# Two PSUM tiles of the first transposes trade places, and one more operand split on VectorE, in a fused attention and two feed-forward layers

## The chip, the cores and the metric

The kernel runs on one core of one Trainium2 chip. The metric is device time in microseconds (us), the median of three runs. A core has TensorE (PE: matmuls; PEld: the loading of their weights), VectorE (DVE), ScalarE (ACT), GpSimd (POOL) and SyncE (SP, which here issues nearly all DMAs). Matmul results land in PSUM, which has eight banks of 128 partitions by 512 float32 values.

## The reference

Float32 data of 2 batches, 12 heads, 448 positions and 64 values a head; 896 tokens of 768 values behind the attention.

```
# attention, for each batch and head
scores = cap * tanh((q @ k.T / sqrt(64)) / cap)
attn   = exp(scores - max); attn = attn / (sum(attn) + 1e-9)
x      = attn @ v                        # heads side by side: 896 x 768
# first feed-forward, d_ff 1024
h    = x @ w_in
solu = h * softmax(h)
ln   = (solu - mean(solu)) / sqrt(var(solu) + 1e-6) * g_ln
x2   = ln @ w_out
# second feed-forward, d_ff 1536
out  = (silu(x2 @ w_gate) * (x2 @ w_val)) @ w_out2
```

## The kernel before, in words

Every matmul operand is split into two parts, hi (a rounded copy, made by an ACT Copy or a DVE CAST) and lo (the remainder, a DVE subtraction), and a product is three matmuls: hi by hi, hi by lo, lo by hi. The attention goes over 12 pairs of heads (6 in each batch). For pair `i`, `attn_T` (L198) transposes q and k on TensorE into PSUM and writes their hi and lo parts to the tile `ks_i`; `attn_qk` (L222) makes the scores `sc` in four chunks, each followed by a tanh on ScalarE into the tile `P`; one exp over all of `P`; `attn_sums` (L243) makes the softmax sums in the tile `S_i`; `attn_pv` (L268) multiplies with v; `attn_norm` (L279) writes the split result to the tile `x`. `attn_pair` (L290) interleaves them: scores of pair `i`, transposes of pair `i+1`, sums and values of pair `i-1`, and beside them the conversion of one slice of `w_in` (tile `wi`, on VectorE). In this part each engine runs its instructions in the order in which the code is written.

Before the first pair, TensorE runs 18 small matmuls on zeros (`keep_warm`, L174, tile `warm`); then the seven transposes of q of pair 0 (tile `T_q`), two more zero matmuls, and the seven of k (`T_k`). The hi parts of pair 1's k and q are made on VectorE, those of all other pairs on ScalarE.

The attention's PSUM is two pools. The pool of the scores has banks 0 to 3 (two tiles of two banks). The other, `ptA`, has one slot for each tag: `pv`, `S` and `t`. A slot is as large as the largest tile of its tag (two banks for `t`, since `T_1` and all later pairs take k and q in one tile of two banks), and the slots lie in the order in which the tags are first used. `pv` comes first (the zero matmuls write into it), then `S` (for `T_q`), then `t` (for `T_k`): in the built program `pv` is bank 4, `S` bank 5, `t` banks 6 and 7.

The first feed-forward goes over seven blocks of 128 tokens. `ff1_h` (L357) makes `h` of a block in 36 matmuls, alternating between two halves of 512 columns. Its `tail` follows: on VectorE the maximum (TENSOR_REDUCE), on ScalarE the exp, on VectorE the product with `h` (SCALAR_TENSOR_TENSOR, the last reader of `h`), the statistics, one step on GpSimd, and a TENSOR_SCALAR that writes the normalised block to the tile `e`. `ff1_T` (L422) then transposes `e` (tiles `lt`). The order on TensorE is: `h` of block 0, `h` of block 1, `lt` of block 0, `h` of block 2, `lt` of block 1, and so on. `h` of block 0 starts inside the attention's last pair and takes a tile of the tag `t` (`htag`). From block 1 on, both PSUM pools are given back and one pool of eight single banks is used; a tile in it waits for whatever last used its bank. In the built program, of before and of the change, it gives the halves of block 1 banks 0 and 7, the two `lt` tiles of block 0 banks 6 and 5, and the halves of block 2 banks 4 and 3.

Of the kernel before, what the change touches and what calls it, by code (L numbers as in the profile page):

```python
# [5 lines left out]
F32 = mybir.dt.float32  # L6
# [30 lines left out]
class Kernel:  # L37
# [160 lines left out]
    def attn_T(self, i):  # L198

        CP, S = self.CP, self.S  # L200
        r = self.raws[i]
        ks = r["ks"] = self.at.tile([128, 2, 2, S], F32R, name=f"ks_{i}", tag="ks", bufs=2)
        if i:
            ps = self.pt.tile([128, 2, 512], F32, name=f"T_{i}", tag="t")
            lots = [(ps, "kq", S)]
        else:
            ps = [self.pt.tile([128, 512], F32, name=f"T_{n}", tag=t) for n, t in (("q", "S"), ("k", "t"))]
            lots = [(p.unsqueeze(1), n, w) for p, n, w in zip(ps, "qk", (S, CP))]
        for ps, names, w in lots:
            for c in range(7):  # L210
                for j, n in enumerate(names):
                    a = slice(0, 64) if n == "k" else slice(64, 128)
                    self.transpose(ps[:, j, c * 64:(c + 1) * 64], r["kq"][a, c * 128:(c + 1) * 128], self.ident[a, a])
            m = slice("kq".index(names[0]), "kq".index(names[-1]) + 1)
            for a in (slice(0, w), slice(w, S)):
                if a.start < a.stop:
                    (self.hi_dve if i == 1 else self.hi_act)(ks[:, m, 0, a], ps[:, :, a])
                    self.lo_dve(ks[:, m, 1, a], ps[:, :, a], ks[:, m, 0, a])
            if names == "q":
                self.keep_warm(2)  # L220

    def attn_qk(self, i, c):  # L222

# [444 lines left out]
```

## Time and profile before

| | |
|---|---|
| median of 3 runs | 507.58 us (506.9 to 508.31) |
| the profiled execution, its own time | 507.78 us |
| its span, first to last instruction | 506.0 us |
| TensorE busy | 493.0 us (97%) |
| VectorE busy | 352.3 us (70%) |
| ScalarE busy | 248.7 us (49%) |

The span is what the trace shows; the execution's own time has 1.78 us around it. Busy shares are means over stages with different limits: about 112 us of attention, then the first feed-forward to about 241 us, then the second to the end.

### The profile page before, as it was taken

The page shows a single profiled execution, that of the slowest core. Times are in us where ns is not written, and L with a number is a line of the kernel's source. Part 1 is how long each engine was busy: PE and PEld are TensorE (multiplying, and loading weights), DVE is VectorE, ACT ScalarE, POOL GpSimd, SP SyncE. Part 2 cuts the span into 40 slices and gives each one's busy share as a digit, 9 for nine tenths or more (in the row PEclk, how much of TensorE's full clock was granted, in tenths as well). Part 3 has the DMA queues.
Part 4 walks back from the last instruction along what each step waited for, and adds up shares of the span by engine and source line. Part 5 has one row for each costly group of instructions (what it writes and reads, how often), then busy time and mean ns, then how long its engine had stood idle before and what let it go on. Part 6 is the DMA issues. An engine that isn't in the chain of part 4 may idle for free.

```text
span 506.0 us, 7801 instructions
## 1 busy us (share of the span) xinstructions
PE 493.0 (97%) x3112; PEld 406.6 (80%) x3112; DVE 352.3 (70%) x634; ACT 248.7 (49%) x362; POOL 21.8 (4%) x62
## 2 busy tenths in 40 slices
PE   8999999995999999999999999999999999999997
PEld 7544454544888899988999988899999889999996
DVE  2799999975387896668899989897997868200000
ACT  5999999841212697466544444343444434100000
POOL 1111111110000000000000000000000000000000
PEclk9999999998899999999999999999999999999999
DMA  6865655220000232145444544534343534000000
GB/s 148 214 164 145 151 143 138 62 79 6 0 1 0 72 95 82 46 127 185 145 160 133 177 135 145 168 126 149 105 152 95 155 96 155 32 31 32 31 33 31
DMA packets 66694, 52.42 MB, mean 104 GB/s; under 512 B 35681, under 2 KB 62049, under 8 KB 66657
## 3 DMA queue, kind: packets, MB, share of 16 engines
q1 hardware_dynamic: 66624, 51.92, 35.4%
q8 instruction: 24, 0.39, 0.3%
q14 instruction: 14, 0.11, 0.1%
q0 software_dynamic: 32, 0.00, 0.0%
HBM read 49.16 MB, written 2.75 MB: 103 GB/s over the span
## 4 chain that ended last, share of the span: by engine, by line
PE 93%; ACT 5%; DVE 1%; issue 0%; ACTq 0%
PE o L29 17%; PE g L29 17%; PE v L29 17%; PE h L29 12%; PE x L29 11%; PE pv L29 7%; PE sc L29 6%; ACT P L29 4%; PE S L29 4%; PE lt L29 1%; PE warm L29 1%; DVE sm L29 1%; ACT e L29 0%; DVE e L29 0%; ACT wo L29 0%
## 5 line engine op out<-in xcount | busy, mean ns | idle before, releaser
L29 PE MATMUL g<-x,y 128*128 128x512 f32 (+1 forms) x432 | 91.2, 363 | 0.0
L29 PE MATMUL v<-x,y 128*128 128x512 f32 (+1 forms) x432 | 90.5, 362 | 0.0
L29 PEld LDWEIGHTS g<-x,y 128*128 128x128 f32 x432 | 78.4, 188 | 8.9
L29 PEld LDWEIGHTS v<-x,y 128*128 128x128 f32 x432 | 78.2, 188 | 8.5
L29 PE MATMUL h<-wi,x 128*128 128x512 f32 x252 | 61.3, 403 | 5.5 <-DVE e L29 5.5
L29 PEld LDWEIGHTS h<-wi,x 128*128 128x128 f32 x252 | 48.4, 194 | 17.0 <-DVE e L29 5.9
L29 PE MATMUL o<-x,a 128*128 128x384 f32 x294 | 52.3, 334 | 0.0
L29 PEld LDWEIGHTS o<-x,a 128*128 128x128 f32 x294 | 51.1, 188 | 0.0
L29 ACT ACTIVATE P<-sc,consts 112x896 f32<-112x896 f32 x48 | 45.9, 1012 | 6.2 <-PE sc L29 6.1
L29 PE MATMUL sc<-ks 64*112 64x448 f32 x288 | 38.8, 387 | 2.5 <-ACT P L29 1.1
L29 ACT ACTIVATE P<-P,consts 112x3584 f32<-112x3584 f32 x12 | 39.5, 3289 | 0.4
L517 ACT ACTIVATE ob<-o 128x384 f32<-128x384 f32 x14 | 6.9, 490 | 64.6 <-PE o L29 64.6
L29 PE MATMUL pv<-P,v 112*32 112x448 f32 x384 | 38.3, 539 | 0.0
L29 PEld LDWEIGHTS sc<-ks 64*112 64x112 f32 x288 | 22.4, 171 | 19.2 <-ACT P L29 8.3
L29 PE MATMUL x<-lB,wo 128*128 128x256 f32 (+1 forms) x192 | 37.3, 338 | 0.4 <-ACT lB L29 0.4
L29 PE MATMUL o<-y,a 128*128 128x384 f32 x189 | 34.1, 334 | 0.0
L29 PEld LDWEIGHTS o<-y,a 128*128 128x128 f32 x189 | 32.9, 188 | 0.1
L29 PEld LDWEIGHTS x<-lB,wo 128*128 128x128 f32 x192 | 30.1, 189 | 3.6 <-ACT lB L29 0.6
L29 PEld LDWEIGHTS pv<-P,v 112*32 112x32 f32 x384 | 12.4, 110 | 23.9 <-issue 23.1
L29 PE MATMUL x<-lA,wo 128*128 128x384 f32 x144 | 28.5, 336 | 0.0
L29 PEld LDWEIGHTS x<-lA,wo 128*128 128x128 f32 x144 | 25.2, 188 | 1.1
L29 DVE SCALAR_TENSOR_TENSOR w<-w_raw,w 128x768 uint32<-128x768 uint32 (+1 forms) x26 | 23.1, 891 | 0.3
(96 smaller groups left out, 623.5 us busy)
## 6 DMA issues: line engine op xcount, KB each, us to landing
wg_raw<-in_moe_w_gate_dram SPq DMA_DIRECT2D x12, 768.0 KB, 4.2
wv_raw<-in_moe_w_val_dram SPq DMA_DIRECT2D x12, 768.0 KB, 4.2
w_raw<-in_moe_w_out_dram SPq DMA_DIRECT2D x11, 768.0 KB, 4.4
wi_raw<-in_moe_w_in_dram SPq DMA_DIRECT2D x12, 512.0 KB, 5.0
wo_raw<-in_moe_w_out_dram SPq DMA_DIRECT2D x12, 512.0 KB, 3.5
kq<-in_q_dram SPq DMA_DIRECT2D x24, 112.0 KB, 4.6
kq<-in_k_dram SPq DMA_DIRECT2D x24, 112.0 KB, 2.7
v<-in_v_dram SPq DMA_DIRECT2D x24, 112.0 KB, 2.6
```

The source lines that it names most:

```text
L29: i = f(*a, **k)
L517: nc.scalar.activation(ob, acc, AF.Copy)
```

## The change

```diff
-            ps = [self.pt.tile([128, 512], F32, name=f"T_{n}", tag=t) for n, t in (("q", "S"), ("k", "t"))]
+            ps = [self.pt.tile([128, 512], F32, name=f"T_{n}", tag=t) for n, t in (("q", "t"), ("k", "S"))]
...
-                    (self.hi_dve if i == 1 else self.hi_act)(ks[:, m, 0, a], ps[:, :, a])
+                    (self.hi_dve if i in (1, 2) else self.hi_act)(ks[:, m, 0, a], ps[:, :, a])
                     self.lo_dve(ks[:, m, 1, a], ps[:, :, a], ks[:, m, 0, a])
-            if names == "q":
-                self.keep_warm(2)
```

All of it is in `attn_T`. `T_q` takes the slot `t` and `T_k` the slot `S`, so that the tags are first used in the order `pv`, `t`, `S`: in the built program `t` is now banks 5 and 6, and `S` bank 7. The two zero matmuls between the first q and k are gone. The hi parts of pair 2's k and q are made on VectorE.

TensorE where block 1 of the first feed-forward begins, before (`h_0` is block 0, `h_1_0` and `h_1_1` are the halves of block 1, `lt_0_1` the second transposed half of block 0; what stands in brackets names the engine whose semaphore is waited for):

```order
L29 MATMUL h_0_1353<-wi0_123,x_125 128x512 x2
L29 MATMUL h_1_0_1531<-wi0_123,x_125 128x512
L29 MATMUL h_1_1_1532<-wi0_123,x_125 128x512 [waits DVE_49]
L29 MATMUL h_1_0_1531<-wi1_124,x_125 128x512
L29 MATMUL h_1_1_1532<-wi1_124,x_125 128x512
...
L29 MATMUL lt_0_0_1587<-ident_102,e_0_1498 128x128 [waits DVE_49]
L29 MATMUL lt_0_0_1587<-ident_102,e_0_1498 128x128 x3
L29 MATMUL lt_0_1_1594<-ident_102,e_0_1498 128x128 [waits PE_49]
```

The same place after the change:

```order
L29 MATMUL h_0_1350<-wi0_123,x_125 128x512 x2
L29 MATMUL h_1_0_1528<-wi0_123,x_125 128x512
L29 MATMUL h_1_1_1529<-wi0_123,x_125 128x512 [waits PE_49]
L29 MATMUL h_1_0_1528<-wi1_124,x_125 128x512
L29 MATMUL h_1_1_1529<-wi1_124,x_125 128x512
...
L29 MATMUL lt_0_0_1584<-ident_102,e_0_1495 128x128 [waits DVE_49]
L29 MATMUL lt_0_0_1584<-ident_102,e_0_1495 128x128 x3
L29 MATMUL lt_0_1_1591<-ident_102,e_0_1495 128x128 x4
```

The order of the matmuls is the same. The first matmul of the second half of block 1 waited for VectorE, and now for TensorE's own earlier work; `lt_0_0` waits for VectorE in both.

VectorE in pair 1 of the attention, from the lo parts of pair 1's operands (`ks_204`, `ks_201`) to the transposed sums of pair 0 (`tr`), before:

```order
L29 TENSOR_TENSOR ks_204<-T_205,ks_204 128x2x448
L29 TENSOR_SCALAR wi_240<-wi_raw 128x512
L29 TENSOR_SCALAR wi_240<-wi_240 128x512 x2
L29 SCALAR_TENSOR_TENSOR wi_240<-wi_raw,wi_240 128x512 x2
L29 TENSOR_TENSOR ks_271<-T_272,ks_271 128x2x448
L29 STREAM_TRANSPOSE tr_315<-S_306 128x448
```

and after:

```order
L29 TENSOR_TENSOR ks_201<-T_202,ks_201 128x2x448
L29 TENSOR_SCALAR wi_237<-wi_raw 128x512
L29 TENSOR_SCALAR wi_237<-wi_237 128x512 x2
L29 SCALAR_TENSOR_TENSOR wi_237<-wi_raw,wi_237 128x512 x2
L29 CAST ks_268<-T_269 128x2x448
L29 TENSOR_TENSOR ks_268<-T_269,ks_268 128x2x448
L29 STREAM_TRANSPOSE tr_312<-S_303 128x448
```

The CAST of pair 2 stands between the conversion of the first `w_in` slice and the lo part that needs it; on ScalarE the Copy that did the same is gone from between the second and the third tanh of pair 1.

## Rows read from the trace of the kernel before

**Rows 1.** The page: span, and the bounding engine's busy time

```profile
span 506.0 us, 7801 instructions
...
PE 493.0 (97%) x3112; PEld 406.6 (80%) x3112; DVE 352.3 (70%) x634; ACT 248.7 (49%) x362; POOL 21.8 (4%) x62
```

**Rows 2.** Waits of TensorE: who for whom, total us, times, longest

```profile
PE h L29 <- DVE e L29: 5.5, 1, 5.5
```

**Rows 3.** Chain that ended last, by time: start, us, what

```profile
118.99 1.30 DVE sm L29 x2
...
124.67 10.45 PE h L29 x35
...
135.99 8.18 PE h L29 x36
```

**Rows 4.** Timeline from block 0's tail on: start, us, instruction, idle before

```profile
123.88 0.73 DVE L29 SCALAR_TENSOR_TENSOR e<-e,sm,h 128x512 f32<-128x512 f32 x1
...
126.77 0.81 DVE L29 TENSOR_SCALAR e<-e,sm 128x1024 f32<-128x1024 f32 x1
134.73 1.02 PEld L29 LDWEIGHTS lt<-ident,e 128*128 128x128 f32 x8
134.93 1.29 DVE L29 TENSOR_REDUCE sm<-h 128x1 f32<-128x512 f32 x2 [7.35 <-PE h L29]
134.96 1.03 PE L29 MATMUL lt<-ident,e 128*128 128x128 f32 x8
...
142.95 0.81 DVE L29 TENSOR_SCALAR e<-e,sm 128x1024 f32<-128x1024 f32 x1
...
144.01 1.03 PE L29 MATMUL lt<-ident,e 128*128 128x128 f32 x8
```

**Rows 5.** Stretches: length, busy PE, PEld, DVE, ACT, POOL, PEclk granted, DMA

```profile
112.00:119.00 7.00, 7.00 (x31) 5.58 (x31) 3.25 (x8) 0.00 (x0) 0.59 (x3) 1.00 0.23 75
119.00:124.67 5.67, 0.18 (x2) 0.00 (x1) 3.98 (x9) 1.45 (x4) 0.00 (x0) 0.82 0.00 0
124.67:127.00 2.33, 2.33 (x6) 1.85 (x7) 1.48 (x5) 0.00 (x0) 0.56 (x1) 0.50 0.00 0
129.00:131.00 2.00, 2.00 (x9) 1.58 (x9) 0.00 (x0) 0.00 (x0) 0.00 (x0) 0.90 0.00 0
153.00:180.00 27.00, 27.00 (x133) 22.58 (x130) 22.93 (x52) 14.08 (x35) 1.10 (x2) 1.00 0.16 46
```

**Rows 6.** The same chain in its first 18 us

```profile
5.09 0.94 PE T_q L29 x7
6.03 0.62 PE warm L29 x4
6.65 0.59 PE T_k L29 x7
...
8.48 1.01 ACT P L29
...
16.64 0.86 PE sc L29 x6
```

**Rows 7.** Groups of weight loads from 5 to 7.5 us: count, busy us, mean ns, idle

```profile
L29 PEld LDWEIGHTS T_q<-ident,kq 64*128 64x128 f32 x7 | 0.8, 215 | 0.1
L29 PEld LDWEIGHTS T_k<-ident,kq 64*128 64x128 f32 x7 | 0.5, 137 | 0.1
```

**Rows 8.** Timeline of pair 1 of the attention: VectorE, and TensorE's next scores

```profile
11.80 1.09 DVE L29 CAST ks<-T 128x896 fp32r<-128x896 f32 x1 [2.95 <-PE T L29]
...
15.36 0.43 DVE L29 TENSOR_SCALAR wi<-wi_raw 128x512 uint32<-128x512 uint32 x1 [1.34 <-DMA wi_raw<-in_moe_w_in_dram]
...
16.74 1.42 DVE L29 SCALAR_TENSOR_TENSOR wi<-wi_raw,wi 128x512 uint32<-128x512 uint32 x2
...
18.32 1.09 DVE L29 TENSOR_TENSOR ks<-T,ks 128x896 fp32r<-128x896 f32 x1 [0.16 <-ACT ks L29]
...
23.00 1.48 PE L29 MATMUL sc<-ks 64*112 64x448 f32 x12
```

## The prediction

> **What bounds the kernel now.** I read the page first: TensorE is busy 493.0 of 506.0 us [rows 1], so a change can only win by taking away matmul time, by filling one of the few holes in it, or by what the clock does around a hole. The list of TensorE's waits shows where the holes are: one of them, 5.5 us, is in front of a matmul of `h` and ends with VectorE's work on `e` [rows 2]. The chain of waits gives its place. The last matmul of block 0's `h` ends near 118.99, the chain then goes through block 0's tail on VectorE and ScalarE, and comes back to TensorE at 124.67 [rows 3]. The timeline says what was waited for: the second product with `h` starts at 123.88 and takes 0.73, so it ends at 124.61, and the matmul starts 0.06 later [rows 4]. Nothing that block 1 computes with is made there. That product is merely the last reader of `h` of block 0, which lies in banks 6 and 7, and the second half of block 1 was given bank 7.
>
> The stretches by time show a second loss behind the first. The granted clock is 1.00 before the hole, 0.82 on the mean inside it, 0.50 when the matmuls start again, and 0.90 between 129 and 131 [rows 5]: TensorE stood still, its clock fell from 2.4 to 1.2 GHz, and it came back only after some 4.7 us of work. With the clock at full in the last part of 129 to 131, 0.90 means 0.4 us at half, so half clock lasted from 124.67 to about 129.4. The chain agrees: 35 matmuls of block 1 take 10.45 us where 36 of block 2 take 8.18 [rows 3]; 35 at that pace are 7.95, so 2.5 us were lost to the clock.
>
> **The change part by part.** All times are those of the trace of before; what moves at the start moves all of it.
>
> *The banks.* After the change `h` of block 0 is in banks 5 and 6, and bank 7 belongs to the sums, whose last reader comes long before 118.99. The wait of the second half of block 1 is now for TensorE's own earlier work. So block 1 follows block 0 without a stop, and at the pace of block 2 (8.18 us) it ends at 118.99 + 8.18 = 127.17. Next in TensorE's order are the transposes of block 0, and these need the true result of the tail: the TENSOR_SCALAR that writes `e` ends at 126.77 + 0.81 = 127.58 [rows 4]. With the 0.06 seen above, the weight load starts at 127.64; before, the first matmul followed its weight load by 134.96 - 134.73 = 0.23 us, and I take 0.15 to 0.2, so the transposes start at 127.8. They started at 134.96. The gain is 7.2 us, which holds 5.5 of the hole and 2.5 of the clock less a new, short hole of 0.6. This is what is late next.
>
> Bounds of this term: if the tail were done in time, 134.96 - 127.17 = 7.8. If block 0's tail goes as slowly as block 1's did, with matmuls and transposes beside it (134.93 to 142.95 + 0.81 = 143.76, so 8.83 instead of 8.59) [rows 4], `e` is there at 127.82, the transposes start at 128.1, and the gain is 6.9.
>
> One step further the same question comes again. VectorE starts block 1's tail right after `e` of block 0, at 127.6, and with 8.83 it is done at 136.4. TensorE reaches block 1's transposes at 127.8 plus the 9.05 of before (144.01 - 134.96), at 136.85. There is some 0.4 us to spare, and from there on every block stands to its tail as it did before. Behind that nothing holds the shift back: between 153 and 180 VectorE is busy 22.93 of 27 us, TensorE all of it, and the DMA share is 0.16 [rows 5], so what VectorE and ScalarE do there comes at TensorE's pace and moves with it.
>
> *The two zero matmuls.* They hold TensorE from 6.03 to 6.65, and the transposes of k, ScalarE's Copy, the first scores and the row of tanh that keeps ScalarE in the chain from 8.48 to 16.6 all follow them [rows 6]. Without them k's transposes start at 6.03. What the trace does not show is their pace there. Weight loads of one shape take 215 ns for q and 137 for k [rows 7]: TensorE is still slow when q goes through and fast when k does. At their own 0.59 the transposes end 0.62 earlier; at q's 0.94 they end at 6.97 instead of 7.24, 0.27 earlier [rows 6]. They now lie across the change of pace, so I take 0.4, and keep 0 (if k's data should be late) and 0.62 as bounds. ScalarE carries it on to the scores at 16.64, where TensorE becomes the chain.
>
> The Trainium skill, TensorE: Matmul & The Clock Gate, "Part 1: The HAM clock gate", says that the warm-up is a budget of time and not a number of matmuls. By it, two matmuls fewer don't bring the fast clock earlier, and this term would be 0.27; the 215 and 137 ns of this trace fit it, but no run here shows it yet.
>
> *Pair 2's hi on VectorE.* ScalarE loses a Copy between two tanh; no TensorE wait hangs on it. VectorE gains a CAST, 1.09 us by pair 1's [rows 8]. VectorE's work there starts at 15.36, when a slice of `w_in` lands, which the change doesn't move. Its product step ends at 16.74 + 1.42 = 18.16; then the CAST to 19.25, then the lo part to 20.34, against 18.32 + 1.09 = 19.41 before [rows 8]. TensorE wants pair 2's operands at 23.00, or 22.6 with the shift: 2.2 us to spare. So it costs nothing; without that cover each microsecond late would be one of TensorE's.
>
> *Sum.* 7.2 + 0.4 = 7.6 us off the profiled execution's 507.78 (span 506.0 and 1.78 around it): 500.2. The median of the runs is 0.2 lower, so I predict 500.0. With the terms' bounds the gain is 6.9 to 8.4, and the runs of before lie 1.4 us apart: the likeliest case's own range is 499.1 to 501.2.
>
> **The rivals.**
>
> A, the forecast: 0.75.
>
> B, the clock's part isn't won: 0.10. Either the clock falls in the changed kernel too, at the new short hole, or the timed runs of before lost less to it than the profiled one. Against the first: the new hole is a tenth of the old one, and in the old one the mean was still 0.82. For the second: the hole is one and the same length in each run, yet the clock's fall may be early, late or absent in it. Then the gain is 7.6 - 2.5 = 5.1 and the time 502.5. The same section of the Trainium skill says that the chip's activity window runs free of the kernel, so that the moment of the change differs from run to run; that is this rival, and the 1.4 us between the runs of before leave it room.
>
> C, part is given back in the first feed-forward: 0.07. The tail of block 0 or 1 is later than I reckon, because VectorE and ScalarE now work while TensorE writes PSUM, or the weights of `w_out` are not ready for a TensorE that comes 7 us earlier. For it: VectorE is at 85% from 153 to 180 [rows 5]. Against it: that work too comes behind the tails. Half of the 7.2 lost would be 503.6.
>
> D, slower than before: 0.03. Without the two zero matmuls TensorE has pauses sooner after its start, and the clock falls back or rises late in the attention's first pairs. Each microsecond at half clock costs half a microsecond of matmuls, so from 7.6 / 0.5 = 15.2 us on, that is if half clock lasted from about 7 to beyond 22, the kernel would be slower; to the end of the attention, some 100 us, it would be 42 us slower, near 550. Against it: from then on TensorE has little but work.
>
> E, the change does not do what it says, and block 1 waits for another reader: 0.05. Then only the start is won, 507.2. The order speaks against it, as the only wait left in block 1 is TensorE's own.
>
> **How the numbers follow.** The time is A's, 500.0. The range reaches below to the bound of A with a fast run, 498.8, and above over B, to 502.6; C's worse half, D and E stay out, about 0.13, with the rest of the 0.2 for what isn't listed. About 0.3% (1.5 us) is what a measurement of this kernel can tell from no change. A, B and C are beyond it: 0.92 faster; E gives 0.05 within 0.3%; D 0.03 slower.
>
> **What would show each step.** In the changed kernel's list of waits the 5.5 us of `h` for `e` is gone, and in its place `lt` waits for `e` some 0.4 to 0.8 us, near 127.3. The granted clock stays at 1.00 through that stretch, and the 36 matmuls of block 1 take about 8.2 us. The scores that stood at 16.64 stand at about 16.2. In pair 1 VectorE shows two pieces of 1.09 for `ks` back to back, the second ending near 20.3, and TensorE does not wait for it at 22.6. The prediction is wrong if the clock still falls near 122, if block 1's transposes wait as well (then each tail is late, and the hole is paid again block by block), or if a wait appears at the `w_out` weights behind 180.

## The result, and the profile after

The changed kernel takes 500.44 us in the median of four runs (500.07 to 502.0), the kernel before 507.24 (506.15 to 508.31, four runs with the earlier three). The ratio is 0.9872, 95% interval 0.9848 to 0.9896: 6.8 us off, where 7.6 were forecast. The profiled execution is the slowest of the four, 502.0 with a span of 500.2. Two executions that were disturbed over their whole length are left out of all medians and ratios: one of 1718.46 us, the only one with a trace in the run that puts the zero matmuls back beside the change, and one of 549.72 us of the kernel before in the same round.

First the page (span and busy times) and TensorE's list of waits (who for whom, total us, times, longest), to be held against [rows 1, 2]:

```profile
span 500.2 us, 7793 instructions
...
PE 492.3 (98%) x3108; PEld 406.5 (81%) x3108; DVE 353.2 (71%) x635; ACT 248.0 (50%) x361; POOL 22.0 (4%) x62
```
```profile
PE sc L29 <- ACT P L29: 0.6, 1, 0.6
PE lt L29 <- DVE e L29: 0.5, 1, 0.5
PE T_k L29 <- DMA kq<-in_k_dram: 0.4, 1, 0.4
```

The 5.5 us of `h` are gone. In their place stand 0.5 us of `lt` for the true result `e`, and a wait that was not there before, of `T_k` for its data (0.4 us).

The timeline where the hole was (start, us, instruction, idle before), against [rows 4]:

```profile
113.30 15.25 PE L29 MATMUL h<-wi,x 128*128 128x512 f32 x66
...
120.44 1.29 DVE L29 TENSOR_REDUCE sm<-h 128x1 f32<-128x512 f32 x2 [2.85 <-PE h L29]
...
128.22 0.81 DVE L29 TENSOR_SCALAR e<-e,sm 128x1024 f32<-128x1024 f32 x1
128.94 1.28 DVE L29 TENSOR_REDUCE sm<-h 128x1 f32<-128x512 f32 x2
...
129.09 1.09 PE L29 MATMUL lt<-ident,e 128*128 128x128 f32 x8 [0.53 <-DVE e L29]
...
137.13 0.81 DVE L29 TENSOR_SCALAR e<-e,sm 128x1024 f32<-128x1024 f32 x1
...
138.21 1.03 PE L29 MATMUL lt<-ident,e 128*128 128x128 f32 x8
```

Block 0 and block 1 are now one unbroken piece of 66 matmuls. From block 0's first reduction to the first `lt` it is 129.09 - 120.44 = 8.65 us; before it was 134.96 - 118.99 = 15.97 on the timeline's starts [rows 3, 4]. This is 7.32 us. The next block's `e` ends at 137.94 and its `lt` starts at 138.21 without a wait.

The stretches (columns as in [rows 5]): the clock that was granted stays at 1.00 through the place of the hole.

```profile
119.00:124.00 5.00, 5.00 (x24) 4.14 (x23) 1.95 (x6) 1.45 (x4) 0.00 (x0) 1.00 0.00 0
...
127.00:129.00 2.00, 1.56 (x7) 0.94 (x5) 1.18 (x5) 0.00 (x0) 0.56 (x1) 1.00 0.00 0
```

The start went the other way. The chain of waits in the first 20 us, against [rows 6], and the weight loads from 4.5 to 8 us, against [rows 7]:

```profile
2.84 3.42 DMA kq<-in_k_dram
6.27 0.14 issue
6.40 0.99 PE T_k L29 x7
...
7.74 5.17 PE sc L29 x24
...
18.20 0.86 PE sc L29 x6
```
```profile
L29 PEld LDWEIGHTS T_k<-ident,kq 64*128 64x128 f32 x7 | 0.8, 216 | 0.5 <-issue 0.5
L29 PEld LDWEIGHTS T_q<-ident,kq 64*128 64x128 f32 x7 | 0.8, 215 | 0.1
```

`T_k` should have started at 6.03 and run at some pace between its own and q's, 0.59 to 0.94 us for the seven. It started at 6.40, since the second half of k landed only at 6.27, and it ran wholly at q's pace, 0.99 us. The scores that follow were slow too, and those that stood at 16.64 stand at 18.20: 1.56 us lost, where 0.4 were to be won. The granted clock stands at 1.00 in this trace from its start on, also where weight loads of one shape take 216 ns instead of 137, so the slow stretch cannot be read from that column. TensorE's weight loads for the scores show how long it was slow (timeline of PEld; six loads took 0.82 us and later 0.47):

```profile
11.42 0.82 PEld L29 LDWEIGHTS sc<-ks 64*112 64x112 f32 x6 [0.30 <-ACT P L29]
...
18.20 0.47 PEld L29 LDWEIGHTS sc<-ks 64*112 64x112 f32 x6 [0.76 <-ACT P L29]
```

Pair 2's hi on VectorE is as forecast: two pieces of 1.09, against [rows 8], and TensorE comes 3.9 us after their end (20.65 and 24.56). So much is to spare only because this execution's scores are late: in the third profile of the change, further down, whose scores are early, the same pieces end at 20.16 and TensorE comes at 22.63, 2.5 us later (2.2 were forecast). The change's list of waits also has 0.2 us of `sc` for `ks` on VectorE; that one is at pair 1 (15.87), and stands as well in runs that leave pair 2's hi on ScalarE.

```profile
18.44 1.08 DVE L29 CAST ks<-T 128x896 fp32r<-128x896 f32 x1
...
19.56 1.09 DVE L29 TENSOR_TENSOR ks<-T,ks 128x896 fp32r<-128x896 f32 x1
...
24.56 1.09 PEld L29 LDWEIGHTS sc<-ks 64*112 64x112 f32 x12 [0.73 <-ACT P L29]
```

### The profile page after: what moved, and what is told of

Its sections match the earlier page's. It is cut to its first block, busy times and chain, and to the rows that moved or that the text cites. A ratio compares the mean times of both kernels' runs of the same rounds, so it can differ in the third digit from the quotient of the medians.

```text
span 500.2 us, 7793 instructions
## 1 busy us (share of the span) xinstructions
PE 492.3 (98%) x3108; PEld 406.5 (81%) x3108; DVE 353.2 (71%) x635; ACT 248.0 (50%) x361; POOL 22.0 (4%) x62
## 4 chain that ended last, share of the span: by engine, by line
PE 92%; ACT 5%; DVE 1%; DMA 1%; issue 0%; SPq 0%; POOL 0%; ACTq 0%; POOLq 0%
PE o L29 17%; PE g L29 17%; PE v L29 17%; PE x L29 12%; PE h L29 10%; PE pv L29 7%; PE sc L29 6%; ACT P L29 4%; PE S L29 4%; PE lt L29 1%; DVE sm L29 1%; DMA kq<-in_k_dram 1%; DVE e L29 0%; SPq L196 0%; ACT e L29 0%
## 5 line engine op out<-in xcount | busy, mean ns | idle before, releaser
L29 PE MATMUL h<-wi,x 128*128 128x512 f32 x252 | 58.8, 392 | 0.0
L29 PEld LDWEIGHTS h<-wi,x 128*128 128x128 f32 x252 | 46.9, 188 | 10.5 <-issue 1.1
L29 PE MATMUL sc<-ks 64*112 64x448 f32 x288 | 40.4, 403 | 2.0 <-ACT P L29 0.6
L29 PEld LDWEIGHTS sc<-ks 64*112 64x112 f32 x288 | 23.7, 181 | 18.7 <-ACT P L29 8.8
```

Of the source, the lines that this page charges most:

```text
L29: i = f(*a, **k)
```

## The experiments

All ratios are to the kernel before on the same chip, with 95% intervals. The starts in the table at the end are from each kernel's timeline.

**The slots alone.** The trade of slots without the other two edits:

```diff
-for n, t in (("q", "S"), ("k", "t"))
+for n, t in (("q", "t"), ("k", "S"))
```

> The kernel before with the trade of the two PSUM slots alone; the two zero matmuls and pair 2's Copy on ScalarE stay. Theory 1 (all of the gain is block 1's wait for a bank, and the clock that fell behind it): 7.2 us faster than the kernel before, near 500.0; the 5.5 us wait of h for e is gone, lt waits some 0.5 us for e, the granted clock stays at 1.00 from 112 to 135, and the scores that stood at 16.64 stay at 16.6. Theory 2 (the other two edits carry part of it): less than 6.5 us faster.

500.96 us, ratio 0.9863 (0.9844 to 0.9881), 6.9 us faster. TensorE's waits:

```profile
PE lt L29 <- DVE e L29: 0.5, 1, 0.5
PE T_k L29 <- DMA kq<-in_k_dram: 0.4, 1, 0.4
```

The trade carries the whole gain. But `T_k` waited here too, although the zero matmuls were there, and the scores were at 17.09, not at 16.6. TensorE's clock had been up already for q (138 ns a weight load) and fell again behind the wait (stretches):

```profile
8.00:9.00 1.00, 1.00 (x8) 0.72 (x6) 0.51 (x1) 0.67 (x2) 0.00 (x0) 0.50 0.65 147
```

**The rest alone.** The change without the trade, as edits of the kernel before:

```diff
-(self.hi_dve if i == 1 else self.hi_act)
+(self.hi_dve if i in (1, 2) else self.hi_act)
...
-            if names == "q":
-                self.keep_warm(2)
```

> The change without the trade of slots: no zero matmuls between the first q and k, pair 2's hi on VectorE, banks as before. Theory 1: the 5.5 us wait stays, and the kernel is between 0.4 us faster and 1.6 us slower than before, depending on when TensorE's clock rises: the scores that stood at 16.64 stand at 16.2 if it rises near 6.5 us as before, and near 18.2 if it rises near 13.3 as in the changed kernel's profile. Theory 2: faster by 0.4 us or more in every run, with the scores at 16.2.

508.41 us, ratio 1.0008 (0.9996 to 1.0021). Its twelve executions lie in two groups, 506.9 to 507.3 (four) and 508.4 to 508.9 (eight). The kernel before has such long executions too, only fewer: 5 of its 17 beside it take 508.3 to 509.0. The hole of 5.5 us is as before, and `T_k` waits 0.7:

```profile
PE h L29 <- DVE e L29: 5.5, 1, 5.5
...
PE T_k L29 <- DMA kq<-in_k_dram: 0.7, 1, 0.7
```

**Zero matmuls in the hole.** The kernel before, with TensorE kept busy by matmuls on zeros while it waits, to price the clock by itself.

```diff
         for _, f in h[0][1:]:
             f()
+        self.keep_warm(40)
```

> The kernel before with 40 more zero matmuls on TensorE between block 0's and block 1's h (some 5.3 us of work at full clock, about as long as the hole), banks as before. Theory 1: block 1 still starts near 124.7, but the granted clock stays at 1.00 and its matmuls take 8.2 us, so the kernel is 2.3 to 2.5 us faster than before. Rival (the clock's fall in the hole is met in the profile but not in most timed runs): within 0.7 us of the kernel before.

505.11 us, ratio 0.9949 (0.9934 to 0.9964): 2.6 us faster by the ratio, with nothing useful added. The wait is still there in substance, but filled (stretches, then the timeline of PE):

```profile
118.00:122.00 4.00, 4.00 (x64) 3.65 (x63) 1.92 (x6) 1.45 (x4) 0.00 (x0) 1.00 0.00 0
122.00:127.00 5.00, 4.52 (x36) 3.64 (x34) 4.08 (x8) 0.00 (x0) 0.56 (x1) 1.00 0.01 3
```
```profile
118.35 4.88 PE L29 MATMUL warm<-z 128*64 128x64 f32 x80
...
124.14 8.23 PE L29 MATMUL h<-wi,x 128*128 128x512 f32 x35 [0.48 <-DVE e L29]
```

The clock stays at 1.00, and 35 matmuls take 8.23 us instead of 10.45 [rows 3]. So the clock's part was 2.2 us in the profile and 2.6 (1.8 to 3.3 by the interval) in the timed runs, which also hold what the starts differ by (0.45 us in the two profiles). The rival that most runs don't meet it falls: all six runs (504.86 to 505.5) lie below all 17 of the kernel before (506.37 and up).

**Slots and pair 2's hi, with the zero matmuls put back**, as an edit of the changed kernel:

```diff
+            if names == "q":
+                self.keep_warm(2)
```

> The changed kernel with the two zero matmuls put back (slots traded, pair 2's hi on VectorE). Theory 1: the same time as with the slots alone, within 0.3 us, and its runs lie closer together than the changed kernel's 500.07 to 502.0; the CAST ends by 20.4 and nothing on TensorE waits for it. Rival (the zero matmuls are pure cost): 0.4 us slower than the changed kernel's fastest runs, 500.5. Rival (VectorE's extra CAST delays pair 2): a wait of sc for ks on VectorE near 23.

500.26 us (500.13 to 500.37), ratio 0.9852 (0.9831 to 0.9873). The runs were indeed close together, but the interval overlaps those of the slots alone and of the change. No wait of `sc` for VectorE stands in its list.

**Block 0's transposes later.** The slots traded, and the new 0.5 us wait covered with a sixth of block 2:

```diff
-        steps = h[1] + T[0] + h[2] + T[1] + ...
+        steps = h[1] + h[2][:1] + T[0] + h[2][1:] + T[1] + ...
```

> The slots traded alone (two zero matmuls kept, pair 2's Copy on ScalarE), and block 0's transposes moved behind the first sixth of block 2's h (six matmuls, some 1.4 us). Theory (TensorE's 0.5 us wait of lt for e is what is left of the hole, on the path): that wait is gone and the kernel is 0.5 to 0.6 us faster than with the slots alone, near 499.7. Rival (the wait comes back at a later block, since the tails follow each other on VectorE with no slack): lt waits at block 1, and the time stays within 0.2 us of the slots alone.

501.09 us, ratio 0.9879 (0.986 to 0.9897): not faster. The rival had it right:

```profile
PE lt L29 <- DVE e L29: 1.3, 1, 1.3
```

The wait at block 0 is gone and a longer one stands at block 1, whose tail follows block 0's on VectorE without slack. The tail itself got longer too: from its first reduction (127.35) to the end of `e` (137.26) it is 9.91 us, and 9.00 with the slots alone; VectorE now runs half of block 2's reduction (0.68) just in front of block 1's `e` (timeline):

```profile
135.86 0.68 DVE L29 TENSOR_REDUCE sm<-h 128x1 f32<-128x512 f32 x1
136.46 0.80 DVE L29 TENSOR_SCALAR e<-e,sm 128x1024 f32<-128x1024 f32 x1
```

From block 0's first reduction to `g` it takes 115.78 us instead of 115.02 with the slots alone.

**No zero matmuls, nothing else.**

```diff
-            if names == "q":
-                self.keep_warm(2)
```

> The kernel before without the two zero matmuls between the first q and k, nothing else. Theory (they cover k's landing, near 5.7 or near 6.2 us, and keep TensorE busy while its clock rises; without them TensorE waits for the DMA): no gain, between 0.3 us faster and 1 us slower than before; TensorE waits 0.3 to 0.7 us for kq in front of T_k. Rival (my prediction's term): 0.4 us faster.

507.8 us, ratio 1.001 (0.9998 to 1.0023); two groups again, six executions at 506.6 to 507.5 and six at 508.1 to 508.8; of the 17 of the kernel before beside it two take over 508. `T_k` waits 0.6 us, and in this trace the clock had risen and fell again (stretches):

```profile
8.50:11.00 2.50, 2.50 (x14) 1.62 (x14) 0.00 (x0) 1.95 (x3) 0.00 (x0) 0.50 0.73 167
12.00:15.00 3.00, 2.84 (x42) 2.39 (x40) 2.18 (x2) 2.97 (x2) 0.00 (x0) 1.00 1.00 222
```

**Block 1 half by half.** Banks as before, but all 18 matmuls of the half in bank 0 come first.

```diff
-                    for i in range(2):
+                    for i in ((0,) if t == 1 else range(2)):
                         self.PE.matmul(st["h"][i], x, w[:, kk, f[i]], start=s, stop=e)
+                if z and t == 1:
+                    for k2 in range(self.KD):
+                        xh, xl = self.xcols(t, k2)
+                        a, y = k2 == 0, k2 == self.KD - 1
+                        for x, w, s, e in ((xh, wh, a, False), (xh, wl, False, False), (xl, wh, False, y)):
+                            self.PE.matmul(st["h"][1], x, w[:, k2, f[1]], start=s, stop=e)
```

> The kernel before, banks as before; only block 1's h is made half by half (18 matmuls of the half in bank 0, then 18 of the half in bank 7) where the halves alternate now. Theory 1 (only bank 7 was waited for): the first half fills the hole, h waits 1.3 to 1.8 us for e instead of 5.5, the granted clock stays at 1.00, lt does not wait, and the kernel is 6 to 6.5 us faster than before, 500.9. Rival (block 1 waits for all of block 0's tile, or for its data): the wait stays at 5.5 and the time at 507.

501.43 us, ratio 0.9893 (0.9872 to 0.9914). The list of waits and the timeline:

```profile
PE h L29 <- DVE e L29: 1.6, 1, 1.6
```
```profile
123.86 4.38 PE L29 MATMUL h<-wi,x 128*128 128x512 f32 x18 [1.64 <-DVE e L29]
```

Only the half in bank 7 waited: from block 0's first reduction to `lt` it is 9.90 us in place of 15.97, 6.1 won of the trade's 7.3. This is a second way to most of the gain, without touching the slots. Its start is the earliest of all (scores at 15.85), although TensorE stood still for q's data for 0.14 us, which is too short for its list of waits (timeline; the zero matmuls end at 4.71):

```profile
2.75 1.96 PE L29 MATMUL warm<-z 128*64 128x64 f32 x20
4.85 0.61 PE L29 MATMUL T_q<-ident,kq 64*128 64x64 f32 x7
```

**More zero matmuls**, on top of the later transposes:

```diff
-                self.keep_warm(2)
+                self.keep_warm(6)
```

> The slots traded and block 0's transposes moved as in the run with the transposes later, and six zero matmuls between the first q and k instead of two. Theory (a pause before k's transposes lets the clock fall or rise late, at up to 1.5 us): as fast as with two, within 0.4 us, with the runs closer together and no fall of the clock before 20 us. Rival (zero matmuls are pure cost): 0.3 to 0.5 us slower than with two in every run.

501.19 us, ratio 0.9882 (0.9865 to 0.9899). The same time as with two, so the rival of 0.3 to 0.5 us missed; but the runs (500.93 to 502.08) are not closer together, as the theory had it.

**The first k by ScalarE's queue**, on top of the change:

```diff
-                nc.sync.dma_start(...)
+                q = nc.scalar if i == 0 and n == "k" else nc.sync
+                q.dma_start(...)
```

> The changed kernel (no zero matmuls between the first q and k), with the two loads of the first k issued by ScalarE's queue at the start instead of SyncE's behind q. Theory (what the missing zero matmuls cost is TensorE's wait for k, with the clock's late rise behind it): k lands by 5.2 us, TensorE does not wait for kq in front of T_k, the scores that stood at 16.64 before and at 18.20 after stand at 16.0 to 16.4, and the kernel is 0.3 to 0.8 us faster than the changed one. Rival (the clock's rise is by chance, whatever TensorE waits for): the same time as the changed kernel, within 0.3 us, with a late rise in some runs.

500.98 us, ratio 0.9887 (0.987 to 0.9903), the same as the changed kernel beside it (the next run). `T_k` waits no more, but now `T_q` waits 0.2 us, and the scores stand at 17.68:

```profile
PE T_q L29 <- DMA kq<-in_q_dram: 0.2, 1, 0.2
```

The theory missed and the rival came true: the start can be late without a wait for k. Whether the 0.2 us in front of `T_q` did it here is not shown.

**The change once more**, word for word.

> The changed kernel once more, word for word. Theory (k lands near 5.7 or near 6.2 us, and without the zero matmuls TensorE waits for it): again 500.0 to 502.0, and a profile in which TensorE waits 0.1 to 0.7 us for kq before T_k, with the scores anywhere from 16.2 to 18.2, by when the clock rises. Rival (the first profile's late start was a single accident): scores at 16.2 and no run above 500.8.

500.68 us (500.54 to 501.93), ratio 0.9887 (0.9872 to 0.9903). `T_k` waits 0.2 us, runs at 215 ns a weight load, and the scores stand at 18.05. The late start was no single accident.

**The change with the two zero matmuls put back** (the kernel of "slots and pair 2's hi"), **and the change a third time beside it.**

> The changed kernel with the two zero matmuls put back, once more, beside the changed kernel on the same chip. Theory (without them TensorE pauses before its clock has risen, and the rise comes late in a part of the executions): its executions lie 0.3 to 1.0 us below the changed kernel's in the median, its slowest below the changed kernel's slowest by 1 us or more, and sums of pair 0 start by 18.8 us in the profile. Rival (they only take time): 0.1 to 0.4 us above.

> The changed kernel a third time, as the partner of the run with the zero matmuls. Theory: at least one execution 1.2 us or more above its fastest, and the sums of pair 0 start after 18.8 us in the profile, with a pause of TensorE in front of the first k's transposes. Rival: the same executions as its partner, within 0.2 us.

On one chip: with the zero matmuls 500.46 us (three runs, 500.12 to 500.97), ratio 0.9868 (0.9852 to 0.9884); without 500.15 (500.03 to 501.39), ratio 0.987 (0.9853 to 0.9886). No difference in the ratios, so the theory's 0.3 to 1.0 us is not borne out, though intervals of 0.8 us to either side do not exclude it. The changed kernel's slowest run is 1.36 us above its fastest, as the theory had it. With the zero matmuls there is no trace to read. The changed kernel's profile, third time (chain, its first 17 us), paused for k and yet was early:

```profile
2.84 3.24 DMA kq<-in_k_dram
6.08 0.14 issue
6.22 0.63 PE T_k L29 x7
...
16.27 0.87 PE sc L29 x6
```

The starts in all profiles read. "Pause" is how long TensorE stood still for `kq` (by the list of waits; in half by half by the timeline); "sums" the first `S` matmul of pair 0, "max" block 0's first TENSOR_REDUCE, `lt` and `g` the first matmul of each; in us:

| kernel | zero matmuls | pause | sums | max | lt | lt - max | g - lt |
|---|---|---|---|---|---|---|---|
| before | 2 | - | 18.35 | 118.99 | 134.96 | 15.97 | 106.25 |
| the rest alone | 0 | 1.0 | 18.94 | 119.52 | 135.59 | 16.07 | 106.23 |
| no zeros alone | 0 | 0.6 | 18.77 | 119.52 | 136.03 | 16.51 | 106.24 |
| zeros in the hole | 2 | - | 17.90 | 118.46 | 132.21 | 13.75 | 106.27 |
| half by half | 2 | 0.1 | 17.57 | 118.18 | 128.08 | 9.90 | 106.24 |
| slots alone | 2 | 0.4 | 18.79 | 119.39 | 128.04 | 8.65 | 106.37 |
| slots and hi | 2 | - | 18.17 | 118.75 | 127.40 | 8.65 | 106.35 |
| lt later | 2 | - | 18.26 | 118.84 | 128.16 | 9.32 | 106.46 |
| lt later, 6 zeros | 6 | - | 18.28 | 118.88 | 128.20 | 9.32 | 106.43 |
| the change | 0 | 0.4 | 19.91 | 120.44 | 129.09 | 8.65 | 106.32 |
| again | 0 | 0.2 | 19.76 | 120.35 | 129.00 | 8.65 | 106.34 |
| third time | 0 | 0.3 | 17.98 | 118.56 | 127.20 | 8.64 | 106.35 |
| k by ScalarE | 0 | 0.2 | 19.37 | 119.97 | 128.62 | 8.65 | 106.33 |

## Why the prediction was right, point by point

*The banks* (7.2, bounds 6.9 to 7.8): right, 7.32 in the profiles and 6.9 us with the slots alone in the timed runs. `e` was there 8.59 us after the first reduction, as forecast; the transposes followed 0.06 us behind it, their weight load only 0.01 in front of them where 0.15 to 0.2 had been allowed, and that is the 0.1 us more. Its parts are shown apart: the wait was for bank 7 and nothing else (half by half, 1.6 us left of 5.5), and the clock's share was 2.2 us by the trace with the hole filled. The prediction had 2.5, with 7.95 us for 35 matmuls at full clock where the trace has 8.23, so its parts added up to 7.4 (5.5 and 2.5 less 0.6) and not to its 7.2; the measured ones, 5.5 and 2.2 less 0.5, come to 7.2. What is late next came where it was put, 0.5 us of `lt` for `e`, and could not be covered by moving `lt`, because block 1's tail has no slack behind block 0's. Behind `lt` nothing was given back: from `lt` to `g` every kernel takes 106.2 to 106.5 us.

*The two zero matmuls* (0.4 won, bounds 0 to 0.62): this step failed in sign. Without them TensorE gets to k's transposes before k has landed and pauses. In the table, all five profiles without a pause have the sums by 18.35; of the eight with one, six have them between 18.77 and 19.91, and two are early, at 17.57 and 17.98. The six late ones are of two kinds. In three (slots alone, the rest alone, no zeros alone) q's weight loads took 138 ns, so the clock had risen, and it fell back to 0.50 from about 7 or 8 us to about 11. In the other three (the change, again, k by ScalarE) k's took 215 or 216 ns, so it had not risen yet. That the pause is the cause in each is argued from this table and not shown: the two early ones and the run with k by ScalarE's queue leave room for chance. I had taken k's lateness as a reason for winning nothing, and had the clock's late rise only as a rival for a far greater loss (D); a small piece of that rival is what happened. In the timed runs it is less: 0.1% slower for this edit alone, with an interval that reaches no change, and none with the slots traded. What differs there is how many executions are long. With the hole kept, 14 of 24 without the zero matmuls take over 508 us, and 7 of 34 of the kernel before beside them. With the slots traded, 3 of 13 of the changed kernel take 501.4 to 502.0, and none of 11 with the zero matmuls (slots alone, slots and hi) is above 501.0. How much of this is the start no traces show. By how much the edit costs in the mean stays open, and so does what decides in which execution the clock rises early.

The Trainium skill, TensorE: Matmul & The Clock Gate, "Part 1: The HAM clock gate", had it that fewer matmuls don't bring the fast clock earlier, as its budget is one of time: the changed kernel's trace agrees, with k's weight loads at 216 ns. The 0.27 us that the prediction worked out from it did not come, as `T_k` began at 6.40 for want of data and not at 6.03. The same section of the Trainium skill says that the moment of the change differs from run to run for one kernel, since its window runs free; the changed kernel's three profiles agree, with the scores at 18.20, 18.05 and 16.27.

*Pair 2's hi on VectorE* (0): right, no wait of TensorE for it, and 2.5 us to spare where the start was early (2.2 forecast).

The sum of 7.6 came out as 6.8: the banks' 7.3 less about half a microsecond at the start, and the two terms cannot be told closer than the runs' spread. In the profiles it is 5.8 of span, 7.3 won and 1.5 lost at the start. That the time came so near in spite of the second term's sign is owed to that term's smallness, and does not speak for it.

Rival B (the clock not won) fell by the zeros in the hole, but its second half, that some runs lose less there, holds in part. The time from the first reduction to `lt` differs in the three kernels that keep the hole as it was, 15.97, 16.07 and 16.51 us. And in nine of the 49 later runs of the kernel before the granted clock over the whole execution was 0.997 in the mean, not 0.989 to 0.993; eight of the nine are among the fastest, 506.18 to 506.61 us. None of them has a trace, so what they lost in the hole stays open. C fell by the constant time from `lt` on, E by the list of waits, and D's size (a slower kernel) by the result.

## What to carry to other kernels

A wait that the trace puts down to another engine's work may be for the memory that this work still reads, not for its result: ask whether the waiting instruction needs the value, and if it does not, give it another buffer or put work that needs no such buffer in front of it. A hole in front of TensorE can cost more than its length: here 2.2 us on top of 5.5, since the matmuls behind it started at half clock. Filling it with matmuls on zeros prices that part by itself. Work that looks like waste at the start may hide a load's landing, as the two zero matmuls did in the run with the transposes later (q's transposes ended at 6.03 us, k landed near 6.04), and its removal is to be priced with that load's landing time, not with the work's own length.

## What the runs showed that I had not expected

Where TensorE paused for 0.1 to 1.0 us in all within its first 6.5 us, the first sums came as late as 19.91 us; without a pause, by 18.35. The second half of the first k, issued at about the same time in each trace, does not land at the same time (view of DMA issues, the one issued at 2.84; the last column is us to landing; first the kernel before, then the changed one):

```profile
kq<-in_k_dram SPq DMA_DIRECT2D x1, 112.0 KB, 2.8
...
kq<-in_k_dram SPq DMA_DIRECT2D x1, 112.0 KB, 3.4
```

It is 2.8 to 3.2 us in the five profiles without a pause, 3.2 to 3.4 in the six that paused for k, with the two zero matmuls (slots alone, 3.3) or without. So the pause, too, hangs in part on when k happens to land.
